# The last output row of a fused attention and gated feed-forward kernel, stored in three column parts instead of two

## The chip, the cores and the metric

The kernel runs on one core of a Trainium2 chip. The metric is the device time of one execution in microseconds; the median of three runs is given with the lowest and the highest. The core's engines appear in the profile under short names: PE (TensorE, matrix products; PEld is its loading of weights), DVE (VectorE), ACT (ScalarE), POOL (GpSimd) and SP (SyncE, which here only issues transfers).

## The reference

Attention over 4 batches, 8 heads, 768 tokens and a head dimension of 64, in which a query sees only the keys that fall into the same hash bucket, and after it a feed-forward layer with a gate and a gated residual:

```python
q_bits = (np.einsum('bhsd,dk->bhsk', q, proj) > 0)      # 6 bits; the same for k
mask = q_bucket[:, :, :, None] == k_bucket[:, :, None, :]
scores = np.where(mask, scale * q @ k.T, -1e9)
attn = softmax(scores) @ v                              # -> x, 3072 x 512
g, val = x @ w_gate, x @ w_val                          # 512 -> 1536
ffn_out = (gelu(g) * val) @ w_out                       # 1536 -> 512
res_gate = 1 / (1 + exp(-(x @ w_res)))
out = x + res_gate * ffn_out                            # float32
```

## The kernel before

The four batches follow one another. For each, the attention runs in chunks: PE computes scores (L437), ACT takes the exponential (L442), PE multiplies by the values (L411). The result, the layer's input x, stays in SBUF in two forms: `x_tok`, tokens on partitions, and `x_sb`, turned. Then `gate_val(b)` computes the hidden layer `hh` in 12 blocks of 128 features (PE L456, gelu on ACT L475, product on DVE L476). Last comes `project(b)`, a generator with one step for each matmul. For the first three batches its steps are spread between the attention chunks of the next batch; for the last batch nothing is left to spread them over, and the loop at the very end of the kernel runs them one after another. Order on each engine is that of the program text (a manual schedule).

`project(b)` goes over T = 6 tiles of 128 tokens, called rows here. For one row:

- four matmuls (L488) compute x @ w_res into `rps`, and ACT takes the tanh of half of it into `th` (L492), since sigmoid(r) is (tanh(r/2) + 1) / 2;
- twelve matmuls (L502), one for each block of `hh`, accumulate the 512 output columns in `fps`;
- DVE forms (th + 1) * fps in place (L506), and then 0.5 * fps + x into the tile `o` (L509);
- SP stores `o` to the output (L511).

The row's output may be cut into column parts: (k0, k1) counts blocks of 128 columns (KM = 4 of them in all, P = 128). All rows but the last of the last batch are one part, (0, 4). The last row of the last batch is cut. Each part has its own twelve matmuls, its own pair of DVE operations and its own store; `o` and `th` are shared by the parts, but each part asks for its own `fps`:

```python
if b < B - 1:
    fps = mm_ps.tile([P, DMODEL], FP32, tag="f", name="fps")
else:
    fps = sc_ps.tile([P, DMODEL], FP32, tag="sp", name="fps")
```

The pool `sc_ps` is in PSUM and has two slots for the tag "sp" (`bufs=2`), each of 1024 float32 columns; the slots go round in turn, and a slot is given out again when what used it before is done. In the last batch the rows' `fps` tiles thus alternate between two slots. The pool of `o` has two slots as well.

Of the kernel before, what the change touches and what calls it, by code (L numbers as in the profile page):

```python
# [17 lines left out]
def kernel(  # L18
# [18 lines left out]
    KM = DMODEL // P  # L37
# [444 lines left out]
    def project(b):  # L482
        hh = hidden[b]
        for t in range(T):
            last = b == B - 1 and t == T - 1
            rps = mm_ps.tile([P, DMODEL], FP32, tag="r", name="rps")
            for kk in range(KM):
                nc.tensor.matmul(rps, x_sb[b][:, kk, t, :], wr[:, kk, :],  # L488
                                 start=(kk == 0), stop=(kk == KM - 1))
                if kk == KM - 1:  # L490
                    th = g_pool.tile([P, DMODEL], FP32, tag="th", name="th")
                    nc.scalar.activation(th, rps, AF.Tanh, scale=0.5)  # L492
                yield
            o = o_pool.tile([P, DMODEL], FP32, tag="o", name="o")
            for k0, k1 in ((0, 3), (3, 4)) if last else ((0, KM),):
                cs = slice(k0 * P, k1 * P)
                if b < B - 1:
                    fps = mm_ps.tile([P, DMODEL], FP32, tag="f", name="fps")
                else:
                    fps = sc_ps.tile([P, DMODEL], FP32, tag="sp", name="fps")  # L500
                for m in range(KF):
                    nc.tensor.matmul(fps[:, cs], hh[:, m, bass.ts(t, P)], wo[:, m, cs],  # L502
                                     start=(m == 0), stop=(m == KF - 1))
                    if m < KF - 1:
                        yield
                nc.vector.scalar_tensor_tensor(fps[:, cs], th[:, cs], 1.0, fps[:, cs],  # L506
                                               op0=ALU.add, op1=ALU.mult)
                f3, o3 = (x[:, cs].rearrange("p (k n) -> p k n", n=P) for x in (fps, o))
                nc.vector.scalar_tensor_tensor(o3, f3, 0.5, x_tok[b][:, k0:k1, t, :],  # L509
                                               op0=ALU.mult, op1=ALU.add)  # L510
                nc.sync.dma_start(out_t[b, t][:, cs], o[:, cs])  # L511
            yield
# [285 lines left out]
    for s in range(NSLOT - 1, LAST):  # L798
# [12 lines left out]
        if slot == NSLOT - 1:  # L811
            begun = None
            values(*pending.pop(0))
            if b == 0:
                nc.scalar.activation(table, warm[:, 0:1], AF.Gelu)
                begun = [gv_mm(0, 0, wg, 0, KM - 1)]
                values(*pending.pop(0))
                begun.append(gv_mm(0, 0, wv, 0, KM - 1))
                x_turn(b, HP - 1)
                hashed((HP + 2, HP + 3), 0, 3)  # L820
            else:
                mlp_mm(4)
                flush()
                mlp_mm(5)
                x_turn(b, HP - 1)
                mlp_mm(NMM)
            done[0] = 0
            gate_val(b, begun)
            mlp.append(project(b))
# [33 lines left out]
```

## Time and profile before

| | |
|---|---|
| median of 3 runs | 341.63 us (341.53 to 342.25) |
| profiled execution, its own time | 341.95 us |
| its span | 340.2 us, 7585 instructions |
| PE busy | 334.5 us, 98% |
| DVE busy | 215.2 us, 63% |
| ACT busy | 209.9 us, 62% |
| POOL busy | 171.2 us, 50% |
| TensorE clock granted | 1.0 of full speed over the whole span |

Times within the profile are microseconds from the start of the span. A row of the timeline reads: start, duration, engine, line, operation, output and inputs, their sizes, how many, and in brackets how long the engine sat idle before and what ended it. In the chain of waits each piece is the work that the end depended on; "issue" there is time in which the engine waited for nothing that the profile shows. Matmuls are pipelined, so one lasts longer than the distance from its start to the next one's.

### The profile page before, as it was taken

The page shows a single profiled execution, that of the slowest core. Times are in us where ns is not written, and L with a number is a line of the kernel's source. Part 1 is how long each engine was busy: PE and PEld are TensorE (multiplying, and loading weights), DVE is VectorE, ACT ScalarE, POOL GpSimd, SP SyncE. Part 2 cuts the span into 40 slices and gives each one's busy share as a digit, 9 for nine tenths or more (in the row PEclk, how much of TensorE's full clock was granted, in tenths as well). Part 3 has the DMA queues.
Part 4 walks back from the last instruction along what each step waited for, and adds up shares of the span by engine and source line. Part 5 has one row for each costly group of instructions (what it writes and reads, how often), then busy time and mean ns, then how long its engine had stood idle before and what let it go on. Part 6 is the DMA issues. An engine that isn't in the chain of part 4 may idle for free.

```text
span 340.2 us, 7585 instructions
## 1 busy us (share of the span) xinstructions
PE 334.5 (98%) x3060; PEld 203.2 (60%) x3060; DVE 215.2 (63%) x414; ACT 209.9 (62%) x241; POOL 171.2 (50%) x214
## 2 busy tenths in 40 slices
PE   8999999999999999999999999999999999999995
PEld 5668665565666655565666665566566665566443
DVE  6778666464364867777688776877586344343343
ACT  4889973337999872225999992223999994322220
POOL 3899840340458360868999970678889000000000
PEclk9999999999999999999999999999999999999999
DMA  7979999969786332506298541904163521000012
GB/s 234 375 143 199 275 239 173 175 101 203 222 192 191 79 121 67 105 2 138 83 254 244 152 110 69 141 0 76 19 148 79 101 56 64 0 0 2 31 64 93
DMA packets 69715, 42.70 MB, mean 126 GB/s; under 512 B 47920, under 2 KB 66736, under 8 KB 69680
## 3 DMA queue, kind: packets, MB, share of 16 engines
q1 hardware_dynamic: 63264, 36.97, 44.8%
q0 software_dynamic: 6336, 5.24, 10.3%
q8 instruction: 24, 0.39, 0.5%
q14 instruction: 11, 0.09, 0.1%
q10 hardware_dynamic: 80, 0.00, 0.0%
HBM read 29.56 MB, written 6.29 MB: 105 GB/s over the span
## 4 chain that ended last, share of the span: by engine, by line
PE 92%; ACT 3%; DVE 3%; issue 1%; POOL 0%; DVEq 0%; ACTq 0%; POOLq 0%
PE sp L456 35%; PE fps L502 18%; PE sp L437 17%; PE av L411 10%; PE rps L488 6%; ACT e L442 3%; PE hs L208 2%; DVE hh L476 1%; PE hs L237 1%; PE wps L151 1%; PE pt L312 1%; DVE nat L227 1%; PE pt L395 1%; DVE hv L266 0%; PE av L379 0%
## 5 line engine op out<-in xcount | busy, mean ns | idle before, releaser
L442 ACT ACTIVATE e<-sp 128x1024 bf16<-128x1024 f32 x144 | 143.4, 1026 | 12.6 <-PE sp L437 7.1
L259 POOL TENSOR_TENSOR pr<-ld,projt 128x768 f32<-128x768 f32 x48 | 86.5, 1811 | 42.0 <-DVE hv L266 41.2
L475 ACT ACTIVATE gt<-sp 128x768 bf16<-128x768 f32 x48 | 38.9, 810 | 89.5 <-PE sp L456 89.5
L437 PE MATMUL sp<-aug,aug 71*128 71x256 bf16 (+1 forms) x384 | 85.8, 325 | 0.4 <-ACT e L442 0.2
L502 PE MATMUL fps<-wo,hh 128*128 128x512 bf16 (+2 forms) x300 | 79.4, 370 | 0.0
L476 DVE TENSOR_TENSOR hh<-gt,sp 128x768 bf16<-128x768 bf16 x48 | 45.8, 955 | 46.0 <-PE sp L456 43.9
L456 PE MATMUL sp<-x_sb,wv 128*128 128x512 bf16 (+1 forms) x384 | 70.4, 326 | 0.4 <-DVE hh L476 0.4
L456 PE MATMUL sp<-x_sb,wg 128*128 128x512 bf16 (+1 forms) x384 | 70.4, 326 | 0.1
L411 PEld LDWEIGHTS <-e 128*128 128x128 bf16 x1152 | 52.7, 97 | 28.9 <-issue 1.2
L411 PE MATMUL av<-va,e 128*128 128x65 bf16 x1152 | 57.6, 193 | 0.0
L456 PEld LDWEIGHTS <-wv 128*128 128x128 bf16 x384 | 37.5, 98 | 25.5 <-issue 0.8
L456 PEld LDWEIGHTS <-wg 128*128 128x128 bf16 x384 | 37.0, 98 | 25.5 <-issue 1.2
L266 DVE TENSOR_REDUCE hv<-pr 128x12 f32<-128x768 f32 x48 | 44.4, 934 | 4.1 <-POOL pr L259 4.1
L502 PEld LDWEIGHTS <-hh 128*128 128x128 bf16 x300 | 27.7, 97 | 22.0
L437 PEld LDWEIGHTS <-aug 71*128 71x128 bf16 x384 | 29.4, 97 | 11.1 <-issue 1.7
L506 DVE SCALAR_TENSOR_TENSOR fps<-th,fps 128x512 f32<-128x512 f32 (+2 forms) x25 | 16.9, 674 | 24.8 <-PE fps L502 21.6
L488 PE MATMUL rps<-wr,x_sb 128*128 128x512 bf16 x96 | 28.1, 378 | 0.0
L196 DVE STREAM_TRANSPOSE t<-ld 128x768 f32<-128x768 f32 (+1 forms) x26 | 22.7, 896 | 4.1 <-DMA ld<-in_q_dram 3.2
L492 ACT ACTIVATE th<-rps 128x512 f32<-128x512 f32 x24 | 14.3, 594 | 16.5 <-PE rps L488 16.5
L185 POOL TENSOR_SCALAR nat<-ld 128x768 bf16<-128x768 f32 x15 | 12.4, 830 | 15.3 <-DMA aug<-nat 15.3
L359 DVE RECIPROCAL rec<-av 128x6 f32<-128x6 f32 x32 | 6.1, 189 | 22.1 <-PE av L411 21.3
L360 DVE TENSOR_TENSOR x_tok<-av,rec 128x384 bf16<-128x384 f32 x32 | 17.8, 557 | 1.1
(72 smaller groups left out, 230.9 us busy)
## 6 DMA issues: line engine op xcount, KB each, us to landing
ldv<-in_v_dram SPq DMA_DIRECT2D x16, 384.0 KB, 4.9
out_dram<-o SPq DMA_DIRECT2D x23, 256.0 KB, 2.1
ld<-in_q_dram SPq DMA_DIRECT2D x15, 384.0 KB, 5.9
ld<-in_k_dram SPq DMA_DIRECT2D x15, 384.0 KB, 6.4
wg<-in_moe_w_gate_dram POOLq DMA_DIRECT2D x4, 384.0 KB, 8.1
wv<-in_moe_w_val_dram POOLq DMA_DIRECT2D x4, 384.0 KB, 8.3
wo<-in_moe_w_out_dram POOLq DMA_DIRECT2D x3, 512.0 KB, 6.4
wr<-in_moe_w_res_dram POOLq DMA_DIRECT2D x1, 512.0 KB, 12.3
```

The costliest lines, as they stand in the source:

```text
L196: nc.vector.transpose(t32[p, side][:, sl].rearrange("p c h n -> p (c h n)"), raw[p, side][:, sl].rearrange("p c d -> p (c d)"))
L259: nc.gpsimd.tensor_tensor(pr, raw[x][:, t:t + 2].unsqueeze(2).to_broadcast([P, 2, NBITS, D]), projt.unsqueeze(1).to_broadcast([P, 2, NBITS ...
L266: nc.vector.tensor_reduce(hval[x][:, t:t + 2, :], prod.pop((x, t)), axis=mybir.AxisListType.X, op=ALU.add)
L360: nc.vector.tensor_mul(x_tok[b][:, hp, :, hi * D:(hi + 1) * D], o[:, 0:T, 0:D], rec.unsqueeze(2).to_broadcast([P, T, D]))
L411: nc.tensor.matmul(av[p, hi][:, qt, :], e[:, off:off + P], va[:, hi, jt, 0:D + 1], start=first, stop=(p >= HP and jt == T - 1), skip_group ...
L437: nc.tensor.matmul(sp[:, off:off + nq * P], ks[0:KA, hi * T + jt, :], qs[0:KA, hi * T + qt0:hi * T + qt0 + nq, :], start=True, stop=True)
L442: nc.scalar.activation(e, sp, AF.Exp, scale=float(ALPHA))
L456: nc.tensor.matmul(sp[:, c0:c1], w[:, kk, bass.ts(m, P)], xs[:, kk, c0:c1], start=(kk == 0), stop=(kk == KM - 1))
L475: nc.scalar.activation(gt, sp[:, 0:S], AF.Gelu)
L476: nc.vector.tensor_mul(hh[:, m, :], gt, ps[1][:, 0:S])
L488: nc.tensor.matmul(rps, x_sb[b][:, kk, t, :], wr[:, kk, :], start=(kk == 0), stop=(kk == KM - 1))
L502: nc.tensor.matmul(fps[:, cs], hh[:, m, bass.ts(t, P)], wo[:, m, cs], start=(m == 0), stop=(m == KF - 1))
```

## The change

The last row of the last batch, until now cut into a part of 384 columns and one of 128, is cut into parts of 256, 128 and 128. The arithmetic of each output element is the same. One part more means twelve more matmuls and weight loads on PE (36 instead of 24 for the row, over the same number of columns), six instead of four DVE operations, three stores instead of two, and three `fps` tiles instead of two.

```diff
             o = o_pool.tile([P, DMODEL], FP32, tag="o", name="o")
-            for k0, k1 in ((0, 3), (3, 4)) if last else ((0, KM),):
+            for k0, k1 in ((0, 2), (2, 3), (3, 4)) if last else ((0, KM),):
                 cs = slice(k0 * P, k1 * P)
```

## The prediction

> **What bounds the kernel now.** I read the page first: span 340.2 us, TensorE (PE) busy for 9 tenths of every slice but the first and the last, and a chain that ended last which is PE for 92%. The change touches nothing before the last output row, so I went to the end of the chain of waits, from 325 us on:
>
> ```profile
> PE 92%; ACT 3%; DVE 3%; issue 1%; POOL 0%; DVEq 0%; ACTq 0%; POOLq 0%
> ```
> ```profile
> 333.14 0.86 PE rps L488 x4
> 334.00 1.96 PE fps L502 x12
> 335.96 0.03 issue
> 335.99 0.02 DVEq L506
> 336.01 0.04 issue
> 336.06 0.57 DVE fps L506
> 336.63 0.02 issue
> 336.65 0.56 DVE o L509
> 337.21 0.21 DVE fps L506
> 337.43 0.02 issue
> 337.45 0.29 DVE o L509
> ```
>
> Until 335.96 the end hangs on PE: the twelve 384-column matmuls of the first part. From 336.06 it hangs on VectorE (DVE): four operations without a gap, then the last store. The second part's twelve 128-column matmuls are not in the chain; they are covered. So what sets the end is when the first part leaves PE, plus the DVE work after it. The timeline from 333 to 338 us gives the pieces:
>
> ```profile
> 333.84 2.78 PE L502 MATMUL fps<-wo,hh 128*128 128x384 bf16 x24
> ...
> 336.06 0.56 DVE L506 SCALAR_TENSOR_TENSOR fps<-th,fps 128x384 f32<-128x384 f32 x1 [1.39 <-PE fps L502]
> 336.65 0.56 DVE L509 SCALAR_TENSOR_TENSOR o<-fps,x_tok 128x384 f32<-128x384 f32 x1
> 337.13 0.28 DVE L506 SCALAR_TENSOR_TENSOR fps<-th,fps 128x128 f32<-128x128 f32 x1
> ...
> 337.45 0.29 DVE L509 SCALAR_TENSOR_TENSOR o<-fps,x_tok 128x128 f32<-128x128 f32 x1
> ```
>
> DVE ends at 337.45 + 0.29 = 337.74; the timeline of SP has the last store issued at 337.77, and the issues of the last 20 us have its landing 1.6 us later, 339.37. The remaining 0.83 us to 340.2 is the program's end.
>
> ```profile
> out_dram<-o SPq DMA_DIRECT2D x5, 256.0 KB, 2.0
> out_dram<-o SPq DMA_DIRECT2D x1, 192.0 KB, 1.9
> out_dram<-o SPq DMA_DIRECT2D x1, 64.0 KB, 1.6
> ```
>
> **The pieces of the sum.** PE starts one matmul after another at a pitch: 512 columns 0.216 us (2.59/12, the row before); 384 columns 0.1625 (from 333.84 to 335.79, where the first 128-column row starts, over 12); 128 columns 0.055 (from 335.79 to the last start, 336.40, over 11). At 256 columns I take 0.108, half the 512 pitch; in the gate and value stage eight matmuls, four of 512 and four of 256, take 1.30 us (133.42 to 134.72), which leaves 0.109 for one of 256. The last matmul of a group ends by the model 0.27 (256) or 0.22 (128) after its start, and DVE starts 0.10 after that end (335.96 to 336.06). On DVE an operation on 128 columns takes 0.285 to 0.29, on 384 0.56, so on 256 0.42 by the line between. L509 starts 0.03 after the end of the L506 whose output it reads; the next part's L506 starts 0.08 before the end of L509 (336.65 + 0.56 against 337.13).
>
> **What the change removes: a shorter first part.** PE's twelve matmuls of 256 columns start at 333.84, the last at 333.84 + 11 x 0.108 = 335.03, its end is 335.30, and DVE's first L506 starts at 335.40 instead of 336.06: 0.66 us earlier. By then the other inputs are there: the tanh (L492) runs 334.04 to 334.64, and DVE is free after the row before at 334.67. L506 ends at 335.82, L509 runs 335.86 to 336.28.
>
> **What it adds: a third part, and a wait.** Added are 12 matmuls with weight loads, two DVE operations and one store. Part two's matmuls follow at once, 335.14 to 335.75, end 335.97, ready for DVE at 336.07, before DVE is free at 336.20. Its pair runs 336.20 to 336.49 and 336.52 to 336.81: covered on PE, on the path on DVE.
> Part three is where I choose. Each part takes a new `fps` from sc_ps under tag sp, which has two slots. Part one has one, part two the other (that of the row before, free at 334.67, before 335.14), and part three needs part one's slot again, though it writes other columns. Part one's slot is read until its L509 ends at 336.28. So PE, which would go on at 335.80, waits about 0.5 us in front of part three's first matmul. Nothing but part three is queued behind it, and only DVE's last pair waits for it. The price of such a release is in the chain of waits at 137.65, where a matmul waits for DVE to leave its slot:
>
> ```profile
> 136.68 0.97 DVE hh L476
> 137.65 0.04 issue
> 137.69 0.38 PE sp L456
> ```
>
> So part three's matmuls start at 336.28 + 0.04 = 336.32, the last at 336.32 + 11 x 0.055 = 336.93, end 337.14, DVE's L506 starts at 337.24, L509 at 337.56, and it ends at 337.85. DVE, busy without a gap before, has idled 0.43 us (336.81 to 337.24). Against 337.74 that is 0.11 us later: of the 0.66 won at the front, the wait for the slot and the third pair take back 0.77.
>
> **A rule on the pitch.** The row: 0.055 us for 128 columns with a weight load each, with part one's other matmuls just ahead of them. The Trainium skill (TensorE: Matmul & The Clock Gate, section Back-to-back issue gap) gives about 81 ns for sustained pairs at 128 columns, and about 56 ns only for an isolated gap; this speaks against more narrow matmuls, and by it part three would end 11 x 0.026 = 0.29 us later and the change cost 0.40 instead of 0.11 us. The trace's 0.055 is of this very instruction, so I use it.
>
> **The stores.** SP issues three instead of two, at about 336.31, 336.84 and 337.88; an issue occupies SP 0.33 us (337.24 and 337.77, the latter 0.53 after the former), so none queues. The last carries 64 KB as before. Its 1.6 us to landing were measured with the 192 KB store still moving; now the two before it are 64 KB and over a microsecond older. The trace shows no 64 KB store alone. Upward I bound its landing by the 2.0 of the 256 KB stores (+0.4). Downward: the two last stores' bytes moved from 338.05 to 338.97; the first byte came 0.8 after the issue of the first, so the last store's own could begin at 338.58 and took at most 0.39, which at the 381 GB/s of the best quarter microsecond would be 0.17 (-0.2). I take 1.6, its own row, no change.
> The release could cost more than 0.04: the same place lists 0.20 us of PE idle and 0.38 of weight-load idle, so up to +0.3. The 24 added PE instructions could call for one more instruction fetch; 24 packets of queue q8, marked instruction, are in the page, the last lies between 328 and 329 us, and no wait on PE is tied to any in the last rows, so I cost it at 0, with up to +0.3 by the largest unexplained idle rows in weight loading (0.3 to 0.4, early in the kernel).
>
> **Sum.** +0.11 us with bounds -0.1 to +0.8 if all went badly together; singly -0.1 to +0.5. The profiled execution took 341.95 us (span 340.2, and 1.7 around it), so it would be 342.06. It lies 0.3 above the median of the three runs, 341.63 (341.53 to 342.25), and I put the step on the median: 341.74. About 0.2% (0.7 us) is what a measurement of this kernel can tell from no change, so the forecast is no change.
>
> **Rivals.**
> First, the wait costs nothing: part three's matmuls follow part two's without a stop. Then they run 335.80 to 336.41 and are ready at 336.73, as DVE comes free (336.52 + 0.21); its last pair is 336.73 to 337.02 and 337.05 to 337.34. That is 0.40 us earlier, 341.23. For it: the parts write disjoint columns. Against it: the slot is handed over whole, and the pool has two. The Trainium skill (PSUM — Partial Sum Buffer, section PSUM bank collisions raise a hardware error) says two engines may not touch one bank of the same partitions at once even in different columns; no row here shows that. Even this gain is under 0.2%.
> Second, the slot comes back later than part one's L509, only with part two's pair (336.81). Then PE starts at 336.85 and DVE ends at 338.38: 0.64 later, 342.27. For it: by then DVE has part two's operations queued too. Against: the row at 137.69 waits for one operation and starts 0.04 after it, with another DVE operation (137.55 on) already running.
> Third, on the slower side: part three waits for part one's store to land. Issued at 336.31, landed 1.9 later (192 KB row) at 338.2; PE at 338.25, 1.93 later than forecast: 341.63 + 0.11 + 1.93 = 343.67. It decides once part three's first matmul starts past 336.32 + 0.57 = 336.89. For it: all parts write one `o` tile. Against: in the trace the second part's L509 ran at 337.45 while the first store, issued at 337.24, was in flight, so neither DVE nor the tile waits for a store of other columns, and the store does not read `fps`.
>
> **How the numbers follow.** The slot wait of +0.11: 0.71. No wait (-0.40): 0.09. Slot held through part two (+0.64): 0.08, of which a third passes the bound with the other terms. Held until the store (+2.0): 0.06. Something outside the last row, such as other addresses of the code, unseen here: 0.06, half within the bound. Slower by over 0.2%: 0.06 + 0.03 + 0.02, and 0.02 where several upper ends meet: 0.13. Faster: 0.01 from the last case, 0.05 from a median of few runs whose own spread is 0.2% on top of a small gain: 0.06. Rest 0.81. The range goes from the no-wait case less 0.1 (341.1) to the held slot plus 0.1 (342.4).
>
> **What would show it.** In the changed profile: L502 rows of 256, 128, 128 columns; DVE's first L506 near 335.4; a PE idle of about 0.5 us before part three, released by DVE at L509; DVE idle some 0.4 us before its last pair, ending near 337.85; the last store issued near 337.88. I am wrong if PE has no idle there (first rival), if it starts after 336.8 (second and third), or if the last store's landing differs from 1.6 by more than 0.3.

## The result, and the profile after

The changed kernel takes 342.85 us (median of 6 runs, 342.54 to 343.30) against 341.67 for the one before: a ratio of 1.0033 with a 95% interval of 1.0020 to 1.0046, that is 1.13 us slower. A second comparison on another occasion (run e8 below) gave 1.0024 (1.0015 to 1.0033), 0.82 us. The forecast of no change was wrong. The profiled execution took 342.57 us, its span 340.9. Three words are used below. A semaphore is a counter that an instruction or a finished transfer raises and that another instruction can wait for. A store lands in sixteen pieces, each of which raises its semaphore once; its landing is the last of the sixteen. DRAIN is the instruction that follows SP's last wait for a transfer.

The chain of waits of the changed kernel, from the last row's first matmul on:

```profile
333.73 1.32 PE fps L502 x12
335.05 0.03 issue
335.08 0.02 DVEq L506
335.10 0.04 issue
335.14 0.44 DVE fps L506
335.58 0.02 issue
335.61 0.43 DVE o L509
336.04 0.04 issue
336.08 0.84 PE fps L502 x12
336.93 0.02 issue
336.95 0.31 DVE fps L506
337.26 0.02 issue
337.28 0.29 DVE o L509
```

The slot wait is there: part three's matmuls (336.08) hang on part one's L509, 0.04 us after its end. The timeline of the same kernel gives each engine's idle time in the brackets:

```profile
333.56 2.14 PE L502 MATMUL fps<-wo,hh 128*128 128x256 bf16 x24
...
335.14 0.43 DVE L506 SCALAR_TENSOR_TENSOR fps<-th,fps 128x256 f32<-128x256 f32 x1 [0.75 <-PE fps L502]
...
336.08 0.83 PE L502 MATMUL fps<-wo,hh 128*128 128x128 bf16 x12 [0.38 <-DVE o L509]
...
336.95 0.30 DVE L506 SCALAR_TENSOR_TENSOR fps<-th,fps 128x128 f32<-128x128 f32 x1 [0.39 <-PE fps L502]
337.28 0.29 DVE L509 SCALAR_TENSOR_TENSOR o<-fps,x_tok 128x128 f32<-128x128 f32 x1
```

From the row's first matmul to the end of DVE it is 333.56 to 337.57, 4.01 us, against 333.84 to 337.74, 3.90, before: 0.11 us more, the sum of the prediction. The row itself started 0.28 us earlier in this execution, and other executions of kernels without any edit ahead of it start it between 333.33 (e5) and 334.00 (e8); so kernels are compared from that first matmul on. The loss must come after DVE's end. The issues of the last stores are not it:

```profile
out_dram<-o SPq DMA_DIRECT2D x1, 128.0 KB, 1.7
out_dram<-o SPq DMA_DIRECT2D x2, 64.0 KB, 1.5
```

The last store is issued at 337.60, and its last part has landed at 339.13, 1.53 us on (before: 337.77 to 339.32). But the span before ended 0.92 us after the landing, and this one ends 1.73 after it. SP's waits tell where this goes: SP not only issues transfers, at the end of the program (L858) it also waits for all that is outstanding. A row gives the time waited in all, the number of waits and the longest. Before, then after:

```profile
SPq L858 <- DMA out_dram<-o: 0.3, 2, 0.2
```
```profile
SPq L858 <- DMA out_dram<-o: 1.0, 1, 1.0
```

Before, SP waited 0.3 us in two waits, for the last two stores; after, 1.0 us in one, for the last, which stood at another place in its list of waits. The rows of line L858 on SP, before in 337.8 to 339.32 (until the landing) and 339.33 to 339.45:

```profile
L858 SPq EVENT_SEMAPHORE  x9: 17/28/28, 338.1 to 339.1; - x9
...
L858 SPq EVENT_SEMAPHORE  x1: 28/28/28, 339.3 to 339.3; - x1
L858 SPq DRAIN  x1: 7/7/7, 339.4 to 339.4; - x1
```

and after, in 337.8 to 339.12 (until the landing) and in 339.13 to 340.1:

```profile
L858 SPq EVENT_SEMAPHORE  x2: 17/22/28, 338.0 to 338.1; - x2
...
L858 SPq EVENT_SEMAPHORE  x8: 28/28/28, 339.1 to 339.9; - x8
L858 SPq DRAIN  x2: 7/10/13, 340.0 to 340.1; - x2
```

Before, nine of ten waits were over when the last store landed, and one was left. After, two were over and eight were left. The trace's single instructions say why. The stores' semaphores go round in turn, eight of them (100, 102, 105 to 110), and the end waits stand in a fixed order; most test a second semaphore at once:

```
                          before                    after
                          start   (idle before)     start   (idle before)
wait 117                  338.147                   337.987
wait 118, 116             338.201                   338.052
wait 100, 115             338.262                   339.146  1.066  <- last store lands, 339.129
wait 102, 114             338.327                   339.216
wait 105, 113             338.417                   339.286
wait 106, 112             338.487                   339.675  0.361
wait 107, 111             338.557                   339.758
wait 108, 101             338.932  0.347            339.822
wait 109, 103             339.132  0.172            339.884
wait 110, 104             339.339  0.179 <- 339.322 339.948
DRAIN                     339.412                   340.016
```

Before, the last store had semaphore 110, the last in the list. One store more moves it on to the next in the round, 100, the third wait of ten. Seven waits then follow the landing, at 0.06 to 0.08 us each, and with them a stop of about 0.35 us. That stop lies ahead of the same SP instruction in both columns, number 207 counted from 0: in the column before it passed while the stores were under way. From landing to DRAIN it is 0.09 us before and 0.89 after. So the account from the row's first matmul to the end of the span is +0.11 in the row, -0.02 from DVE's end to the landing, +0.80 in the end waits, +0.01 after: 0.90 us, inside the intervals of both comparisons.

### The profile page after: what moved, and what is told of

Its sections match the earlier page's. It is cut to its first block, busy times and chain, and to the rows that moved or that the text cites. A ratio compares the mean times of both kernels' runs of the same rounds, so it can differ in the third digit from the quotient of the medians.

```text
span 340.9 us, 7567 instructions
## 1 busy us (share of the span) xinstructions
PE 331.4 (97%) x3026; PEld 203.0 (60%) x3072; DVE 215.9 (63%) x416; ACT 210.1 (62%) x241; POOL 170.8 (50%) x214
## 4 chain that ended last, share of the span: by engine, by line
PE 90%; ACT 3%; DVE 3%; issue 2%; DMA 1%; POOL 1%; SPq 0%; DVEq 0%; POOLq 0%; ACTq 0%
PE sp L456 34%; PE fps L502 18%; PE sp L437 17%; PE av L411 10%; PE rps L488 6%; ACT e L442 3%; PE hs L208 2%; PE pt L312 1%; DVE hh L476 1%; DMA ld<-in_q_dram 1%; DVE nat L227 1%; PE pt L395 1%; PE hs L237 0%; DVE hv L266 0%; PE av L379 0%
## 5 line engine op out<-in xcount | busy, mean ns | idle before, releaser
L502 PE MATMUL fps<-wo,hh 128*128 128x512 bf16 (+2 forms) x290 | 74.8, 361 | 1.5 <-DVE o L509 0.4
L456 PE MATMUL sp<-x_sb,wv 128*128 128x256 bf16 (+1 forms) x374 | 69.9, 324 | 0.9 <-DVE hh L476 0.4
L456 PE MATMUL sp<-x_sb,wg 128*128 128x256 bf16 (+1 forms) x376 | 70.0, 325 | 0.5
L502 PEld LDWEIGHTS <-hh 128*128 128x128 bf16 x312 | 28.4, 97 | 21.8 <-issue 0.5
L488 PE MATMUL rps<-wr,x_sb 128*128 128x512 bf16 x90 | 26.4, 378 | 0.4
```

The lines of the kernel that those rows point to most:

```text
L456: nc.tensor.matmul(sp[:, c0:c1], w[:, kk, bass.ts(m, P)], xs[:, kk, c0:c1], start=(kk == 0), stop=(kk == KM - 1))
L488: nc.tensor.matmul(rps, x_sb[b][:, kk, t, :], wr[:, kk, :], start=(kk == 0), stop=(kk == KM - 1))
```

## The experiments

Theory: the loss is the place of the last store in the end waits, with the stop; the third part costs 0.11. Rivals: the third part or its wait costs it all; or any store more costs as much wherever it is. The line numbers of experiments shift by two or three (L858 is L860 or L861). Stores are added by cutting those of earlier rows of the last batch, so PE and DVE keep their work:

```diff
-                nc.sync.dma_start(out_t[b, t][:, cs], o[:, cs])
+                n = {0: 2}.get(t, 1) if b == B - 1 else 1     # e1: row 0 in two
+                for c0, c1 in {1: ((cs.start, cs.stop),), 2: ((0, 256), (256, 512)),
+                               3: ((0, 128), (128, 256), (256, 512))}[n]:
+                    nc.sync.dma_start(out_t[b, t][:, c0:c1], o[:, c0:c1])
```

All runs in one table, stretches in us from the profiles: the row (first matmul to DVE's end), to landing (DVE's end to the last store's landing), end waits (landing to DRAIN), all (first matmul to the end of the span), and the timed ratio with its interval.

| kernel | last semaphore | row | to landing | end waits | all | ratio to before |
|---|---|---|---|---|---|---|
| before | 110 | 3.90 | 1.58 | 0.09 | 6.40 | |
| the change | 100 | 4.01 | 1.56 | 0.89 | 7.30 | 1.0033 (1.0020 to 1.0046) |
| e8, the change again | 100 | 4.01 | 1.56 | 0.89 | 7.30 | 1.0024 (1.0015 to 1.0033) |
| e1, two parts, +1 store | 100 | 3.90 | 1.59 | 0.91 | 7.25 | 1.0025 (1.0015 to 1.0036) |
| e2, three parts, +7 | 110 | 4.01 | 1.67 | 0.08 | 6.58 | 1.0000 (0.9990 to 1.0009) |
| e3, two parts, +8 | 110 | 3.90 | 2.15 | 0.08 | 6.97 | 1.0016 (1.0007 to 1.0025) |
| e11, e3 again | 110 | 3.90 | 2.17 | 0.08 | 6.98 | 1.0017 (1.0007 to 1.0028) |
| e9, two parts, +16 | 110 | 3.90 | 1.58 | 0.08 | 6.38 | 0.9998 (0.9989 to 1.0007) |
| e10, two parts, +12 | 106 | 3.90 | 1.58 | 0.33 | 6.65 | 1.0003 (0.9994 to 1.0012) |
| e4, three parts, +8 | 100 | 4.01 | 1.55 | 0.51 | 6.89 | 1.0016 (1.0008 to 1.0025) |
| e5, own slot, two stores | 110 | 3.53 | 1.58 | 0.09 | 6.03 | 0.9986 (0.9978 to 0.9995) |
| e6, shared slot, two stores | 110 | 4.01 | 1.55 | 0.09 | 6.48 | 1.0000 (0.9991 to 1.0009) |
| e7, own slot, three stores | 100 | 3.53 | 1.56 | 0.87 | 6.78 | 1.0015 (1.0006 to 1.0024) |

**e1: one store more, without the third part.** Expected:

> Two parts as before; the first row of the last batch, 17 us before the end, is stored in two halves (one store more). Theory (end waits): at the end SP waits for eight store semaphores in a fixed order; one store more moves the last store from the last place in that order (semaphore 110) to the first (100), and what SP does after it then comes after the landing. So the time from the last landing to SP's drain goes from 0.09 us to 0.8 to 0.9, and the kernel is 0.7 to 0.9 us slower than before. Rival (third part): the loss is from the third part or its store; this kernel has none and stays within 0.2 us of before. Rival (any store): each added store costs the same 1.1 us as in the change, here too, but without a change in the end waits.

It loses 0.85 us (0.0025 of 341.88) with the row as before, 3.90. SP's rows of L861 (L858 of before) in 339.07 to 340.0, after the landing:

```profile
L861 SPq EVENT_SEMAPHORE  x8: 28/28/28, 339.1 to 339.9; - x8
L861 SPq DRAIN  x1: 13/13/13, 340.0 to 340.0; - x1
```

The end waits alone make nearly the whole loss of the change. The rival of the third part falls.

**e2: the change with seven stores more** (rows 0 to 2 in three, row 3 in two). Expected:

> Three parts as in the change, and seven more stores in the rows before (rows 0 to 2 of the last batch in three pieces, row 3 in two), so that the last store is again on the semaphore waited for last. End waits: from landing to drain 0.1 us again; the whole is 0.1 us (the local sum of the prediction) slower than before, at most 0.3. Third part: still 1.1 us slower than before. Any store: slower by several times 1.1 us.

The time is that of before, though it has eight stores more: the last one is on 110 again. SP's rows of L861 until the landing (338.3 to 339.72), and after it (to 339.83):

```profile
L861 SPq EVENT_SEMAPHORE  x9: 17/28/28, 338.5 to 339.0; - x9
...
L861 SPq EVENT_SEMAPHORE  x1: 28/28/28, 339.7 to 339.7; - x1
L861 SPq DRAIN  x1: 7/7/7, 339.8 to 339.8; - x1
```

By the stretches it should lose 0.18, of which 0.08 is a landing whose last piece came 0.11 us after the other fifteen; the interval, 0.3 us to either side, doesn't tell that from nothing.

**e3 and e11: the control with eight stores more.** Expected of e3:

> Control: two parts as before and eight more stores (rows 0 to 3 of the last batch in three pieces each), so that the last store has the same semaphore as before. End waits: within 0.2 us of before. Third part: the same. Any store: clearly slower.

This missed: 0.55 us slower, with the end waits as short as before (0.08). The loss lies between DVE's end and the landing, 2.15 instead of 1.58. SP has eight instructions more (223 instead of 215), and instruction 207 is now the last store itself: it was issued at 337.96, 0.24 us after DVE's end instead of 0.03. And fifteen of its sixteen landings came by 339.56, the sixteenth at 339.87. Expected of the second run:

> The control with eight more stores once more. Its first profile had the last issue 0.2 us late behind the stop at SP's instruction 207 and one of the sixteen landings of the last store 0.3 us behind the other fifteen. If the stop is what its loss comes from: the late issue again, and 0.2 us slower than before where the late landing does not return, 0.5 where it does.

Both came back: the issue 0.24 us after DVE's end, and the sixteenth landing 0.34 us behind the fifteenth (340.165 and 339.825). In 338.5 to 339.3 of this run one packet of another queue stands among the store's:

```profile
q1 hardware_dynamic: 209, 0.19, 71.5%
q14 instruction: 1, 0.01, 3.8%
```

The trace has this 8 KB packet at 338.93 for 0.49 us, in e3 at 338.60 for 0.53; the last store's packets began at 338.78 in e3. In the profile before it came at 339.57, after the landing. The store moves as 128 packets of 512 bytes. The last eight, a sixteenth of it, start one after another, 21 to 24 ns apart, from 339.13 in e3 and from 339.42 in e11, in both within 0.01 us of the end of the 8 KB packet (339.13 and 339.42). That this packet held up one sixteenth of the store fits both runs and was not tried by itself.

The packet and the stop belong together in the traces. In all thirteen profiles such a packet starts 0.98 to 1.04 us after the end of SP's instruction 206 (1.16 in e4), wherever in the kernel that falls. The same pair stands 128 SP instructions earlier in all of them: a stop of 0.43 to 0.44 us ahead of instruction 79, and an 8 KB instruction packet 0.63 to 0.67 us after that instruction starts. So both losses of e3 come with instruction 207. A fetch of SP's own instructions would fit this; no run tried it.

**e9: sixteen more,** so that instruction 207 falls into an earlier row (those rows in five pieces). Expected:

> Second control: two parts, sixteen more stores (rows 0 to 3 of the last batch in five pieces each), the last store on semaphore 110 as before and SP's instruction 207, with its 0.35 us stop, in one of those rows and no longer among the last. End waits and stop: landing to drain 0.1 us, the last issue not held up, within 0.2 us of before. Rival (each store added costs): slower than the control with eight stores, by 1.0 us or more.

It holds: 0.9998, 6.38 us from the first matmul against 6.40. Sixteen added stores cost nothing that shows, so the rival of any store falls; what the eight of e3 cost is where they put instruction 207 and the packet.

**e10: twelve more** (those rows in four pieces), the last store on the sixth wait of ten. Expected:

> Dose: two parts, twelve more stores (rows 0 to 3 in four pieces), the last store on the fourth semaphore in the order (106), the stop again in an earlier row. End waits: four waits of 0.07 us after the landing, 0.35 from landing to drain against 0.09 and 0.89, 0.3 us slower than before. If only the first place in the order costs: 0.1 from landing to drain and no loss.

The profile has four waits after the one that the landing released, and the DRAIN 0.33 us after the landing:

```profile
L860 SPq EVENT_SEMAPHORE  x5: 28/28/28, 338.8 to 339.1; - x5
L860 SPq DRAIN  x1: 13/13/13, 339.1 to 339.1; - x1
```

The time rose by 0.10 us (-0.2 to 0.4), which tells 0.25 neither from nothing nor from the 0.3 expected; here the profile carries the verdict.

**e4: the change with eight more.** Expected:

> Three parts and eight more stores: the last store is on the semaphore that the changed kernel's last store has, but SP's instructions before the end are 16 more, so that the stop of 0.36 us that both profiles show ahead of SP's instruction 207 comes before the end waits. End waits: 7 waits of 0.07 us after the landing, 0.5 to 0.55 from landing to drain, without the 0.36; 0.6 us slower than before. If the stop goes with the waits and not with the place in the instruction stream, 0.9 from landing to drain and 1.0 slower. Third part: 1.1 us slower than before.

SP has eight instructions more than in the change (225 instead of 217), not the sixteen that were expected; that is enough. Same place in the list as the change, but instruction 207 is the second part's store and not among the waits: 0.51 from landing to DRAIN. SP's rows of L861 after the landing (339.504 to 340.05):

```profile
L861 SPq EVENT_SEMAPHORE  x8: 28/28/28, 339.5 to 339.9; - x8
L861 SPq DRAIN  x1: 7/7/7, 340.0 to 340.0; - x1
```

Nearly all of the difference to 0.89 is the stop (0.36 where SP otherwise idles 0.03 to 0.06 between two waits), which thus goes with the place in SP's instructions and not with the waits. The time, 0.55 us slower (0.27 to 0.86), agrees with 0.49 by the stretches.

**e5, e6, e7: the slot wait and the store count apart.** For a slot of its own part three takes `fps` from mm_ps; for two stores the first part leaves with the second:

```diff
-                if b < B - 1:
+                if b < B - 1 or (last and k0 == 3):        # e5, e7
                     fps = mm_ps.tile([P, DMODEL], FP32, tag="f", name="fps")
 ...
+                if last and k0 == 0:                       # e5, e6
+                    continue
+                ds = slice(0 if k0 == 2 else k0 * P, k1 * P)
-                nc.sync.dma_start(out_t[b, t][:, cs], o[:, cs])
+                nc.sync.dma_start(out_t[b, t][:, ds], o[:, ds])
```

> Three parts of 256, 128, 128 columns; the third takes its fps from the pool mm_ps (tag f, unused in the last batch), so that it waits for no slot, and the first two parts leave in one store of 384 columns after the second, so that there are as many stores as before and the last one is on semaphore 110. End waits plus slot wait (theory): VectorE ends 3.50 us after the last row's first matmul (3.90 before, 4.01 in the change), landing to drain 0.1 us, 0.3 to 0.4 us faster than before. Rival (the third part itself costs): slower than before by 0.5 or more.

> Three parts as in the change with its slot wait, but two stores (the first two parts in one of 384 columns). Theory: 4.01 us from the last row's first matmul to VectorE's end as in the change, landing to drain 0.1 us as before: 0.1 us slower than before, 0.8 to 1.0 faster than the change. Rival (third part): as slow as the change.

> The change with a slot of its own (mm_ps, tag f) for the third part; three stores, the last on semaphore 100. Theory: VectorE ends 0.5 us earlier than in the change (3.50 us after the row's first matmul), landing to drain 0.89 as in the change: 0.4 us slower than before. If the slot wait were what the change lost: as fast as before or faster.

All three hold, though the 0.1 us expected of e6 is too small for its interval (0.3 us to either side). e6 against the change: the same row, one store less, and the loss is gone (a median of 341.96 us, where the change had 342.93 and before 341.96 on the same occasion). e7: without the slot wait the row falls to 3.53, and the kernel is still 0.51 us slower (0.2 to 0.8). e5 has both mended and is 0.48 us faster than before (0.0014 of 341.96; 0.2 to 0.8), the only version that measured faster than both kernels. In its timeline all 36 matmuls run on without a stop, and DVE from part one on:

```profile
333.33 2.81 PE L502 MATMUL fps<-wo,hh 128*128 128x256 bf16 x36
...
335.38 0.42 DVE L509 SCALAR_TENSOR_TENSOR o<-fps,x_tok 128x256 f32<-128x256 f32 x1
335.72 0.29 DVE L506 SCALAR_TENSOR_TENSOR fps<-th,fps 128x128 f32<-128x128 f32 x1
336.04 0.29 DVE L509 SCALAR_TENSOR_TENSOR o<-fps,x_tok 128x128 f32<-128x128 f32 x1
336.25 0.29 DVE L506 SCALAR_TENSOR_TENSOR fps<-th,fps 128x128 f32<-128x128 f32 x1
336.57 0.29 DVE L509 SCALAR_TENSOR_TENSOR o<-fps,x_tok 128x128 f32<-128x128 f32 x1
```

**e8: the change again.** Expected:

> The changed kernel itself once more, for a second profile of its end and a narrower interval. Theory: 0.9 us slower than before by the sum of the two profiles (0.11 in the row, 0.80 after the landing, less 0.03 of landing), landing to drain 0.9 us again with the 0.36 us stop ahead of SP's instruction 207. If the end waits are an accident of one profile, another figure there.

The stretches are those of the first profile to 0.01 us, the stop ahead of 207 included (0.361). The end waits are no accident of one execution.

## Why the prediction was wrong

- *The row.* Right in its pieces: part one's DVE start 1.58 us after the first matmul (1.56 forecast), the release 0.04, 55 ns a matmul in part three ((0.83 - 0.22) / 11), 4.01 in all. The Trainium skill's 81 ns for such pairs (TensorE: Matmul & The Clock Gate, Back-to-back issue gap) doesn't hold here. The idle of PE in front of part three was called 0.5; the profile counts from the modelled end of the matmul before and shows 0.38.
- *First rival, no wait.* Not what the change does; e5 and e7 show what it would have gained, 0.37 us in the row where 0.40 was forecast.
- *Second and third rival, a slot that comes back later.* Excluded by the start of part three 0.04 us after L509.
- *The stores.* The forecast of 1.6 us from issue to landing held (1.53). That none of the three issues queues held too.
- *The step that failed* is the sentence that the remaining 0.83 us after 339.37 is the program's end. It took a constant for what was a list of waits, nine of them covered by the last store's flight and one not. What the third store does there was never costed: not its 0.33 us on SP, but the turn of the eight semaphores, which it moves by one. Measured, that term is +0.80 us; with the row's 0.11 it makes up the loss. The waits were to be had from the profile before: the row of SP's waits at L858 says that two waits for stores, 0.3 us in all, were exposed, and SP's twelve semaphore rows of L858 say that more waits stand in that list. Of the 0.80 about 0.33 is the stop ahead of instruction 207. The prediction looked for instruction packets on the side of PE alone (queue q8) and put them at 0; queue q14, whose packets come with SP's stop, it did not cost.
- *The range* reached to 342.4 for a slot held longer, and left out the true 342.85; slower was given 0.13, for other mechanisms. The upper bound of the sum is also too small by its own terms: +0.11 with +0.4 for the landing, +0.3 for the release and +0.3 for a fetch makes +1.11 and not +0.8. Even that would have ended at 342.74. None of the three signs of being wrong came up, because none looked behind the landing.

## What to carry to other kernels

What comes after the last transfer is not a constant: look at the end waits instruction by instruction, and ask which are covered only because the last transfer is the last in their list. A transfer added anywhere, even 17 us earlier, can move the last one to another place in that list, and here that cost seven times what the edit did where it was made (0.80 against 0.11 us). An edit that cuts work finer so that the end comes earlier should first free the finer pieces of a shared slot, and keep the number of transfers, or look where the last one then stands (sixteen more, two full turns, cost nothing in e9).

## What the runs showed of the hardware that was not expected

- SP stops 0.35 to 0.36 us ahead of its instruction 207, whatever that is: an end wait (before, the change, e1, e5 to e8) or a store (e3, e4, e9, e11), and in e2 the wait ahead of a store; in e10 a longer wait for DVE (1.64 us) covers it. An 8 KB instruction packet follows, and the same pair stands at instruction 79. What the stop is, the traces do not show.
- An end wait whose semaphores are met takes SP 0.06 to 0.09 us, the stop aside.
- One of sixteen landings of a 64 KB store came 0.31 and 0.34 us after the other fifteen, in the two profiles (e3, e11) in which an 8 KB instruction packet overlapped it.
- The start of the last row varies between 333.33 and 334.00 us among executions whose programs are the same up to it (before, the change, e5 to e8), and between 333.56 and 334.00 for the changed kernel alone, more than some of the effects that were looked for; stretches from the row's first matmul on were reproducible to about 0.01 us (the change and e8; e3 and e11).
